# List-scheduled attention and two feed-forward layers on one core: costs read from a trace, and a rule that keeps GpSimd and VectorE's two-operand SBUF work apart

## The chip, the core and the metric

One core of a Trainium2 chip runs the whole program. The metric is device time in microseconds (us). The times below are those of the kernel before; the profile is of one execution. The engines are called PE (TensorE, matmuls), DVE (VectorE), ACT (ScalarE), POOL (GpSimd) and SP (SyncE, which here only issues DMAs).

## The reference

Causal attention with 2 x 12 heads, 448 positions and 64 values per head, then two feed-forward layers, each 768 to 2048 to 768 on the 896 rows:

```python
scores = scale * np.matmul(q, k.transpose(0, 1, 3, 2))
scores = np.where(mask, -1000000000.0, scores)
attn = np.exp(scores - np.max(scores, axis=-1, keepdims=True))
attn = attn / (np.sum(attn, axis=-1, keepdims=True) + 1e-09)
x = np.matmul(attn, v)                  # heads side by side: 896 x 768
h = x @ w_in;  x = (h * np.clip(h + 3.0, 0.0, 6.0) / 6.0) @ w_out
h = x @ w2_in; y = (np.maximum(h, 0.0) + alpha * np.minimum(h, 0.0)) @ w2_out
```

## The kernel before

**Attention** is cut into 12 units (`attend`, line 273), each of two heads ("sides") of one batch. For a unit PE makes the scores in four steps (`score(0)` to `score(2)` and `score_rest`, lines 286 to 302; tiles `s...` and `sl`). DVE applies the mask and takes the row minimum of the negated scores, seven times (`highest`, line 316, profile line 318). ACT exponentiates each of the seven pieces in place (`exps`, profile line 323). When all seven are there, DVE inverts the row sums (`invert`, lines 331 to 334), and POOL multiplies the seven pieces by the inverse in SBUF (line 338, tiles `el` and `e`): one instruction for `el` and six for the `e` pieces. PE then transposes the 16 blocks into four PSUM banks `t` (lines 345 and 353), each bank is copied to SBUF as a quarter of `a` by ACT or DVE (`copy`, line 374, profile line 375), and PE multiplies by V into `o` (line 387). A unit's `o` is turned into the operands of the first layer by `take_x` (line 242): a copy, or sums and differences with other units (`combine`, profile line 239), each split into a high part rounded by ACT (`split`, line 221) and a low part, a difference made by DVE (line 222).

**The layers** use a seven-product scheme for 2 x 2 blocks in place of eight, and each product is three matmuls (high x high, high x low, low x high) in `three` (line 397; instruction line 404). One such step is three matmuls of 448 columns. The steps of `w_in` (line 411) number 8 groups x 7 products x 3, those of `w_out` (line 496) 192 per layer. All 720 of both layers are chained in one fixed order (`chain="moe"`). The weights arrive as 64-bit integers' words: `convert` (line 196) takes two ACT steps (lines 205 and 207) and two DVE steps (lines 209 and 212) for each tile of 768 columns. In `w_in` the converted tiles are added and subtracted (`sums`, line 418) and split (`both`, lines 429 and 430). The first group's first product is `a <- a1 x b11`: its operands `b1100`, `b1101` and `b1102` come from units 1, 3 and 5.

**The order of all work** is made by a list scheduler (`Plan.solve`, line 94) before anything is emitted. Every step names its engine (or two, for copies) and a cost in us; `LAG` (line 60) is what an engine's result takes to reach another engine. The scheduler keeps a clock for each engine, and takes again and again the step that can start first; among equals, the one that is due first. Buffers of each class are limited (`SLOTS`, line 541), and a step waits for a free one. The result is one order for each engine's queue; at run time every engine works through its queue in that order, and semaphores hold an instruction until its operands are there. So a cost that is wrong in the table moves instructions, and nothing else. The first costs of interest:

```python
LAG = {PE: 0.20, DVE: 0.10, ACT: 0.10, POOL: 0.12, SP: 0.0}
                    t = max(clock[e], o.ready[e])
                        key = (round(t, 2), o.due, o.index)
            o.out = o.end = clock[e] = t + dict(o.on)[e]
            op([(ACT, 0.62), (DVE, 0.64)], copy, reads=[t], writes=[(a, i)])
            op((POOL, 0.26 + 0.00088 * cols), lambda _, view=view, u=u: nc.gpsimd.tensor_scalar(
```

Of the kernel before, what the change touches and what calls it, by code (L numbers as in the profile page):

```python
# [36 lines left out]
def f32(t):  # L37
    return t.bitcast(F32)
# [21 lines left out]
LAG = {PE: 0.20, DVE: 0.10, ACT: 0.10, POOL: 0.12, SP: 0.0}  # L60
# [3 lines left out]
class Plan:  # L64
# [28 lines left out]

    def solve(self, slots, strict, overlay):
# [21 lines left out]
        clock, landed = dict.fromkeys(LAG, 0.0), 0.0  # L116
# [69 lines left out]
class Kernel:  # L186
# [9 lines left out]
    def convert(self, src):  # L196
# [4 lines left out]
        def words(k):  # L201
            return raw.tile.rearrange("p (n two) -> p n two", two=2)[:, :, k]

        op((SP, 0.06), lambda e: nc.sync.dma_start(out=raw.tile, in_=src), writes=[(raw, "l"), (raw, "h")]).load = (1.6, 2.8)
        op((ACT, 0.85), lambda e: nc.scalar.activation(f32(w.tile), f32(words(1)), AF.Copy, scale=2.0 ** -112),  # L205
           reads=[(raw, "h")], writes=[w])
        op((ACT, 0.87), lambda e: nc.scalar.activation(  # L207
# [3 lines left out]
           reads=[w], writes=[(raw, "l")])  # L211
        op((DVE, 0.87), lambda e: nc.vector.scalar_tensor_tensor(  # L212
            out=w.tile, in0=w.tile, scalar=0x80000000, in1=words(0), op0=ALU.bitwise_and, op1=ALU.bitwise_or),
           reads=[(raw, "l")], writes=[w])
        return w

    def split(self, cls, name, cols, src, key, ps=False):

        nc, op = self.nc, self.plan.op
        hi, lo = Buf(cls, name + "h", cols, F32R), Buf(cls, name + "l", cols, F32R)  # L220
        op((ACT, 0.11 + 0.00094 * cols), lambda e: nc.scalar.copy(hi.tile, src()), reads=[key], writes=[hi])  # L221
        op((DVE, 0.14 + 0.00094 * cols), lambda e: nc.vector.tensor_sub(lo.tile, src(), f32(hi.tile)),  # L222
           reads=[key, hi], writes=[lo])
        return hi, lo

    def copy(self, out, src, key, cols):
        nc = self.nc

        def emit(e):
            (nc.scalar.copy if e == ACT else nc.vector.tensor_copy)(out.tile, src())  # L230

        self.plan.op([(ACT, 0.11 + 0.00096 * cols), (DVE, 0.10 + 0.00104 * cols)], emit, reads=[key], writes=[out])

    def combine(self, name, in0, in1, key0, key1, subtract=True):
# [4 lines left out]
        self.plan.op((DVE, 0.55), lambda e: f(t.tile, in0(), in1()), reads=[key0, key1], writes=[t])  # L239
        return t  # L240

    def take_x(self, layer, c, blk, ps):
# [11 lines left out]
        elif low:  # L254
            x[layer, "b11", j] = self.split("u", "b11" + n, S, src, ps)
# [3 lines left out]
        elif blk:  # L259
            x[layer, "b22", j] = self.split("u", "b22" + n, S, src, ps)  # L260
# [5 lines left out]
        else:  # L266
            x[layer, "b21", j] = self.split("u", "b21" + n, S, src, ps)
# [5 lines left out]
    def attend(self, n, c, blk, due):  # L273
        nc, op, d = self.nc, self.plan.op, self.dram
        kq, v = Buf("kq", "kq", S + 4 * P, F32), Buf("v", "v", 8 * D, F32)
        op((SP, 0.06), lambda e: nc.sync.dma_start(out=kq.tile, in_=d["kq"][n]), writes=[kq]).load = (1.6, 2.2)
        op((SP, 0.06), lambda e: nc.sync.dma_start(out=v.tile, in_=d["v"][n]), writes=[v]).load = (1.6, 1.2)
# [21 lines left out]
        op((PE, 0.24), score(0), reads=[kq], writes=[(s01[0], 0), (s01[1], 0)], also=[*e01])  # L299
        op((PE, 0.45), score(1), reads=[kq], writes=[(s01[0], 1), (s01[1], 1)])  # L300
        op((PE, 0.66), score(2), reads=[kq], writes=[*s2], also=[*e2])
        op((PE, 0.77), score_rest, reads=[kq], writes=[sl], also=[el])
# [9 lines left out]
        for t, key, off, e, u, cols in todo:  # L312
# [14 lines left out]
            op((DVE, 0.09 + 0.00102 * cols), highest, reads=[key], writes=[part, (small, u)])  # L327
# [8 lines left out]
        op((DVE, 0.36), invert, reads=[(small, 7 + u) for u in range(7)], writes=[(small, 14)])  # L336
        for view, part, u, cols in views:
            op((POOL, 0.26 + 0.00088 * cols), lambda _, view=view, u=u: nc.gpsimd.tensor_scalar(  # L338
# [25 lines left out]
        for i, blocks in enumerate(banks):  # L364
# [6 lines left out]
            op((PE, 0.50), emit, reads=list(dict.fromkeys((el, 0) if i == 3 else key(kc, i, side) for kc, i, side in blocks)),  # L371
# [5 lines left out]
            op([(ACT, 0.62), (DVE, 0.64)], copy, reads=[t], writes=[(a, i)])  # L377

        o = Buf("ps", "o")
        for kc, us in enumerate((0.77, 0.55, 0.34, 0.13)):  # L380
# [30 lines left out]
    def w_in(self, layer, m, src, due):  # L411
# [5 lines left out]
        def sums(out, oh, in0, h0, in1, h1, f, reads):  # L417
            op((DVE, 0.50), lambda _: f(out.tile[:, oh], f32(in0.tile[:, h0]), f32(in1.tile[:, h1])),  # L418
               reads=reads, writes=[(out, oh.start)])
# [7 lines left out]
        def both(name, cols, src, keys):  # L427
            hi, lo = Buf("w", name + "h", DM, F32R), Buf("w", name + "l", DM, F32R)
            op((ACT, 0.08 + 0.00094 * cols), lambda _: nc.scalar.copy(hi.tile[:, 0:cols], src()), reads=keys, writes=[hi])  # L429
            op((DVE, 0.14 + 0.00095 * cols), lambda _: nc.vector.tensor_sub(lo.tile[:, 0:cols], src(), f32(hi.tile[:, 0:cols])),  # L430
               reads=[*keys, hi], writes=[lo])
# [27 lines left out]
        def finish(h, mm, blk, until, ps=None):  # L459
# [3 lines left out]
            if layer == 0:  # L463
                op((ACT, 0.54), lambda _: nc.scalar.activation(t.tile, src(), AF.Relu, bias=0.5, scale=1.0 / 6.0),  # L464
# [4 lines left out]
            else:  # L469
                op((ACT, 0.54), lambda _: nc.scalar.activation(t.tile, src(), AF.Relu, scale=-1.0),  # L470
# [48 lines left out]
    def store(self, layer, c, blk, ps):  # L519
# [3 lines left out]
        self.plan.op((SP, 0.06), lambda _: nc.sync.dma_start(out=out[c, :, blk, :], in_=o.tile), reads=[o])  # L523

    def build(self):
# [5 lines left out]
        op((SP, 0.06), lambda _: nc.sync.dma_start(out=self.alpha, in_=d["alpha"]), writes=[alpha], due=start + 20.0).load = (1.6, 0.4)  # L531
# [124 lines left out]
```

## Time and profile before

| what | us |
|---|---|
| three timed runs | 552.08, 551.77, 548.56 |
| median of the runs | 551.77 |
| the profiled execution | 548.4 |
| its span, first to last instruction | 546.6 |
| PE busy in the span | 528.2 |
| DVE busy | 428.0 |
| ACT busy | 337.9 |
| POOL busy | 53.5 |

The profiled execution took 1.8 us more than its span. Stretches are given in us from the start of the span. Attention fills the stretch up to about 109; the first layer's `w_in` follows up to about 206, its `w_out` up to about 322, then the second layer in the same way. A busy PE in the table is not a PE at full pace: its clock is granted at one of two levels, and the strip and the table of stretches show the mean of the granted clock, 1.00 being full.

### The profile page before, as it was taken

How to read it: one execution, taken by the hardware profiler on the slowest of the kernel's cores; microseconds unless marked ns; L12 is line 12 of the kernel's file. 1: busy time of each engine (PE TensorE's matmuls, PEld its weight loads, DVE VectorE, ACT ScalarE, POOL GpSimd, SP SyncE). 2: the span in 40 equal slices, each digit the busy share in tenths (PEclk: the TensorE clock that was granted, in tenths of full speed). 3: DMA queues.
4: the chain of work that ended last, by engine and by line, in shares of the span. 5: the costliest groups of instructions: out<-in, count | busy, mean ns of one | idle time of the engine just before them, and what ended most of it. 6: DMA issues, size and time to landing. Idle time of an engine off the chain costs nothing.

```text
span 546.6 us, 7448 instructions
## 1 busy us (share of the span) xinstructions
PE 528.2 (97%) x2712; PEld 459.8 (84%) x2712; DVE 428.0 (78%) x773; ACT 337.9 (62%) x627; POOL 53.5 (10%) x97
## 2 busy tenths in 40 slices
PE   5977999999999999999999999999999999999997
PEld 2544566799999999999999998999999999999996
DVE  4888898799999999997641499999999999751002
ACT  5787688756767899946532366676779985631000
POOL 3454573500000000000000000000000000000000
PEclk9879899999999999999999999999999999999999
DMA  8534332003434343356231012334334344730002
GB/s 312 192 98 166 117 112 76 1 20 108 157 119 140 123 145 115 120 201 225 93 111 62 0 59 65 128 124 146 117 121 145 111 144 149 238 118 1 0 17 84
DMA packets 14581, 62.61 MB, mean 115 GB/s; under 512 B 1745, under 2 KB 3281, under 8 KB 14545
## 3 DMA queue, kind: packets, MB, share of 16 engines
q1 hardware_dynamic: 14544, 62.14, 33.1%
q8 instruction: 21, 0.34, 0.2%
q14 instruction: 16, 0.12, 0.1%
HBM read 59.38 MB, written 2.75 MB: 114 GB/s over the span
## 4 chain that ended last, share of the span: by engine, by line
PE 91%; DVE 3%; POOL 3%; ACT 1%; issue 1%; DMA 1%; POOLq 0%; DVEq 0%
PE y L404 42%; PE a L404 20%; PE c L404 10%; PE b L404 5%; PE o L387 5%; PE t L353 3%; PE s L291 3%; POOL e L338 3%; PE sl L297 2%; PE t L345 1%; DMA kq<-kq 1%; ACT e L323 1%; DVE e L318 1%; DVE t L239 0%; POOL el L338 0%
## 5 line engine op out<-in xcount | busy, mean ns | idle before, releaser
L207 ACT ACTIVATE raw<-raw 128x768 uint32<-128x768 uint32 x64 | 58.8, 919 | 40.6 <-DMA raw<-w2i 18.8
L205 ACT ACTIVATE wf<-raw 128x768 f32<-128x768 f32 x64 | 57.1, 903 | 16.1 <-PE y L404 13.5
L209 DVE SCALAR_TENSOR_TENSOR raw<-wf,raw 128x768 uint32<-128x768 uint32 x64 | 61.5, 962 | 2.6 <-ACT wf L205 2.6
L212 DVE SCALAR_TENSOR_TENSOR wf<-wf,raw 128x768 uint32<-128x768 uint32 x64 | 61.2, 957 | 1.5
L222 DVE TENSOR_TENSOR wol<-wf,woh 128x768 fp32r<-128x768 f32 x32 | 30.4, 953 | 21.4 <-PE y L404 17.3
L338 POOL TENSOR_SCALAR e<-e,small 128x384 f32<-128x384 f32 (+2 forms) x72 | 43.6, 628 | 0.0
L230 DVE COPY o<-y 128x448 f32<-128x448 f32 x10 | 6.2, 624 | 43.3 <-PE y L404 43.3
L221 ACT CAST woh<-wf 128x768 fp32r<-128x768 f32 x32 | 26.3, 836 | 21.1 <-PE y L404 13.6
L323 ACT ACTIVATE e<-e,small 128x384 f32<-128x384 f32 (+2 forms) x72 | 35.7, 501 | 2.9 <-DVE small L318 2.7
L353 PE MATMUL t<-ident,e 128*128 128x128 f32 x144 | 25.9, 303 | 4.9 <-POOL e L338 4.9
L318 DVE CUSTOM_DVE_ANT_0 e<-s,mask 128x384 f32<-128x384 f32 (+2 forms) x72 | 26.7, 417 | 2.5 <-PE s L291 1.8
L387 PE MATMUL o<-a,v 128*64 128x448 f32 (+3 forms) x192 | 28.2, 401 | 0.0
L387 PEld LDWEIGHTS o<-a,v 128*64 128x64 f32 (+1 forms) x192 | 13.4, 137 | 17.3 <-issue 10.2
L353 PEld LDWEIGHTS t<-ident,e 128*128 128x128 f32 x144 | 19.2, 155 | 7.8 <-POOL e L338 7.7
L430 DVE TENSOR_TENSOR s12l<-s,s12h 128x768 fp32r<-128x768 f32 x16 | 15.2, 951 | 12.4 <-PE y L404 12.4
L418 DVE TENSOR_TENSOR s<-wf 128x384 f32<-128x384 f32 x32 | 17.8, 555 | 8.3 <-PE y L404 7.7
L291 PE MATMUL s<-kq 64*128 64x384 f32 (+2 forms) x144 | 22.3, 426 | 0.0
L291 PEld LDWEIGHTS s<-kq 64*128 64x128 f32 x144 | 13.0, 197 | 9.9 <-issue 5.6
L429 ACT CAST s12h<-s 128x768 fp32r<-128x768 f32 x16 | 13.3, 832 | 11.5 <-DVE s L418 10.9
L375 DVE COPY a<-t 128x512 f32<-128x512 f32 x23 | 15.5, 686 | 6.1 <-PE t L353 3.0
L375 ACT COPY a<-t 128x512 f32<-128x512 f32 x25 | 13.9, 590 | 9.7 <-PE t L353 8.2
L464 ACT ACTIVATE r<-g 128x448 f32<-128x448 f32 x24 | 13.7, 572 | 8.1 <-DVE g L457 8.1
(649 smaller groups left out, 1648.9 us busy)
## 6 DMA issues: line engine op xcount, KB each, us to landing
raw<-w1i SPq DMA_DIRECT2D x16, 768.0 KB, 5.0
raw<-w1o SPq DMA_DIRECT2D x16, 768.0 KB, 5.2
raw<-w2i SPq DMA_DIRECT2D x16, 768.0 KB, 4.3
raw<-w2o SPq DMA_DIRECT2D x16, 768.0 KB, 4.6
kq<-kq SPq DMA_DIRECT2D x12, 480.0 KB, 4.7
v<-v SPq DMA_DIRECT2D x12, 256.0 KB, 2.8
y_t<-o SPq DMA_DIRECT2D x12, 224.0 KB, 1.9
alpha<-alpha SPq DMA_DIRECT2D x1, 8.0 KB, 6.7
```

The lines of the kernel that those rows point to most:

```text
L205: op((ACT, 0.85), lambda e: nc.scalar.activation(f32(w.tile), f32(words(1)), AF.Copy, scale=2.0 ** -112), reads=[(raw, "h")], writes=[w])
L207: op((ACT, 0.87), lambda e: nc.scalar.activation(words(0), words(0), AF.Copy, bias=-0.4999, scale=2.0 ** -29 * (1 - 2.0 ** -16)), writes=[ ...
L209: op((DVE, 0.87), lambda e: nc.vector.scalar_tensor_tensor(out=words(0), in0=w.tile, scalar=3, in1=words(0), op0=ALU.logical_shift_left, o ...
L212: op((DVE, 0.87), lambda e: nc.vector.scalar_tensor_tensor(out=w.tile, in0=w.tile, scalar=0x80000000, in1=words(0), op0=ALU.bitwise_and, o ...
L222: op((DVE, 0.14 + 0.00094 * cols), lambda e: nc.vector.tensor_sub(lo.tile, src(), f32(hi.tile)), reads=[key, hi], writes=[lo])
L291: nc.tensor.matmul(t.tile[:, off:off + (i + 1) * P], lhsT=kq.tile[rows, S + i * P:S + (i + 1) * P], rhs=kq.tile[rows, 0:(i + 1) * P], star ...
L318: nc.vector.tensor_tensor_reduce(out=view(), in0=t.tile[:, off:off + cols], in1=self.mask[:, at:at + cols], scale=-SCALE, scalar=3.0e38, o ...
L323: nc.scalar.activation(view(), view(), AF.Exp, bias=small.tile[:, u:u + 1], scale=-1.0, accum_out=small.tile[:, 7 + u:8 + u])
L338: op((POOL, 0.26 + 0.00088 * cols), lambda _, view=view, u=u: nc.gpsimd.tensor_scalar(view(), view(), small.tile[:, 14 + u:15 + u], 1.0, A ...
L353: return lambda t: nc.tensor.transpose(t.tile[:, at:at + P], src.tile[:, off:off + P], self.ident)
L387: nc.tensor.matmul(o.tile[side * D:(side + 1) * D, 0:cols], lhsT=v.tile[rows, (2 * kc + side) * D:(2 * kc + side + 1) * D], rhs=a.tile[row ...
L404: nc.tensor.matmul(out, lhsT=lhs.tile[:, w], rhs=rhs.tile, start=start and lhs is hi and rhs is xh, stop=stop and lhs is lo, skip_group_ch ...
```

## The change

The costs and lags in the plan are replaced by others. A step can carry a mark, `port`: all POOL steps have it, and those DVE steps whose two tensor operands both lie in SBUF (the two of `convert`, `sums`, the low parts in `both`, and `split` when its source is not in PSUM). The scheduler keeps one more clock, `port`, and starts a marked step of DVE or POOL only when the last marked one has ended in its plan. No semaphore is added; the mark acts on the order alone. Operations, buffers and their numbers stay. Of the costs a few lines are shown.

```diff
-LAG = {PE: 0.20, DVE: 0.10, ACT: 0.10, POOL: 0.12, SP: 0.0}
+LAG = {PE: 0.20, DVE: 0.12, ACT: 0.15, POOL: 0.10, SP: 0.04}
...
-    def op(self, on, emit, reads=(), writes=(), due=FAR, chain=None, also=()):
+    def op(self, on, emit, reads=(), writes=(), due=FAR, chain=None, also=(), port=False):
 
         o = Op(on if isinstance(on, list) else [on], emit, due)
+        o.port = port or o.on[0][0] == POOL
...
-        clock, landed = dict.fromkeys(LAG, 0.0), 0.0
+        clock, landed, port = dict.fromkeys(LAG, 0.0), 0.0, 0.0
...
                     t = max(clock[e], o.ready[e])
+                    if o.port and e in (DVE, POOL):
+                        t = max(t, port)
...
             o.out = o.end = clock[e] = t + dict(o.on)[e]
+            if o.port and e in (DVE, POOL):
+                port = o.end
...
         op((DVE, 0.87), lambda e: nc.vector.scalar_tensor_tensor(
             out=words(0), in0=w.tile, scalar=3, in1=words(0), op0=ALU.logical_shift_left, op1=ALU.bitwise_or),
-           reads=[w], writes=[(raw, "l")])
+           reads=[w], writes=[(raw, "l")], port=True)
...
-            op([(ACT, 0.62), (DVE, 0.64)], copy, reads=[t], writes=[(a, i)])
+            op([(ACT, 0.48), (DVE, 0.605)], copy, reads=[t], writes=[(a, i)])
```

On DVE, behind the inversion for unit 2 (the unit whose tiles `e_295` to `e_313` POOL multiplies next), before the change: `s_283` and `s_376` are sums of weight tiles, `raw` a weight tile under conversion. The accumulator read that follows each `L318` row is left out.

```order
L333 TENSOR_SCALAR small<-small 128x7
L334 RECIPROCAL small<-small 128x7
L318 ISA e_340,small<-s_333,mask 128x128
L318 ISA e_341,small<-s_334,mask 128x128
L222 TENSOR_TENSOR b1100l<-o,b1100h 128x448
L418 TENSOR_TENSOR s_283<-s_283,wf 128x384
L239 TENSOR_TENSOR t_372<-b_246,o 128x448
L418 TENSOR_TENSOR s_376<-wf,s_283 128x384
L418 TENSOR_TENSOR s_376<-wf 128x384
L209 SCALAR_TENSOR_TENSOR raw<-wf,raw 128x768
L375 COPY a<-t 128x512
L333 TENSOR_SCALAR small<-small 128x7
```

The same place after the change, from the inversion for unit 2 on; the rows of line 323 are unit 3's score work, and the line numbers are those of the changed file (five higher here):

```order
L338 TENSOR_SCALAR small<-small 128x7
L339 RECIPROCAL small<-small 128x7
L323 ISA e_306,small<-s_304,mask 128x384
L323 ISA e_307,small<-s_305,mask 128x384
L244 TENSOR_TENSOR t_338<-b_252,o 128x448
L323 ISA e_343,small<-s_333,mask 128x256
L323 ISA e_344,small<-s_334,mask 128x256
L323 ISA e_343,small<-s_333,mask 128x128
L323 ISA e_344,small<-s_334,mask 128x128
L227 TENSOR_TENSOR b1100l<-o,b1100h 128x448
L217 SCALAR_TENSOR_TENSOR wf<-wf,raw 128x768
L380 COPY a<-t 128x512
```

Six DVE instructions for unit 3's scores and two with a PSUM operand now stand where three weight sums and a conversion stood.

On PE, behind unit 3's scores (`s_333`, `s_334`) and ahead of unit 2's transposes, before the change:

```order
L291 MATMUL s_333<-kq 128x128
L291 MATMUL s_334<-kq 128x128
L404 MATMUL a<-b1100h,a1h 128x448
L404 MATMUL a<-b1100l,a1h 128x448
L404 MATMUL a<-b1100h,a1l 128x448
L345 MATMUL t<-ident,el 128x2x64
L353 MATMUL t<-ident,e_295 128x128
```

After the change the transposes follow the scores at once:

```order
L296 MATMUL s_333<-kq 128x128
L296 MATMUL s_334<-kq 128x128
L350 MATMUL t<-ident,el 128x2x64
L358 MATMUL t<-ident,e_222 128x128
L358 MATMUL t<-ident,e_264 128x128
```

The first product of the layer (`b1100`) has left this place; it now stands on PE behind the last scores of unit 11, and the second (`b1101`) behind unit 10's first product with V, where before it stood ahead of unit 4's transposes.

On ACT, at the copies of unit 11's four banks `t`, before the change (the other two copies are on DVE):

```order
L221 CAST b2202h<-o 128x448
L221 CAST t202h<-t_1190 128x448
L375 COPY a<-t 128x512 x2
L221 CAST t302h<-t_1224 128x448
L221 CAST b2102h<-o 128x448
```

After the change all four are on ACT:

```order
L226 CAST t401h<-t_1114 128x448
L226 CAST b2202h<-o 128x448
L380 COPY a<-t 128x512 x4
L226 CAST t202h<-t_1151 128x448
L226 CAST t302h<-t_1170 128x448
```

Over all 12 units ACT has 32 of the 48 copies instead of 25, and DVE 16 instead of 23.

## Rows read from the trace of the kernel before

**Rows 1.** The page: span, busy time of the engines, clock strip (40 slices, tenths)
```profile
span 546.6 us, 7448 instructions
...
PE 528.2 (97%) x2712; PEld 459.8 (84%) x2712; DVE 428.0 (78%) x773; ACT 337.9 (62%) x627; POOL 53.5 (10%) x97
...
PEclk9879899999999999999999999999999999999999
```

**Rows 2.** Busy time by stretch: PE, PEld, DVE, ACT, POOL, granted clock, DMA share, GB/s
```profile
8.00:15.00 7.00, 4.67 (x29) 2.70 (x26) 5.41 (x30) 6.70 (x27) 3.01 (x7) 1.00 1.02 420
15.00:31.00 16.00, 15.15 (x89) 8.86 (x87) 14.86 (x39) 12.13 (x27) 5.11 (x9) 0.89 0.52 185
31.00:46.00 15.00, 11.12 (x58) 6.94 (x58) 11.91 (x25) 10.76 (x26) 11.10 (x14) 0.77 0.15 48
46.00:60.00 14.00, 10.57 (x61) 6.94 (x59) 11.37 (x38) 9.89 (x31) 4.74 (x7) 0.88 0.58 202
60.00:91.00 31.00, 31.00 (x217) 18.35 (x216) 28.02 (x97) 26.14 (x79) 18.95 (x35) 1.00 0.35 107
91.00:107.00 16.00, 16.00 (x112) 11.79 (x111) 13.18 (x42) 13.37 (x39) 8.08 (x15) 1.00 0.00 1
107.00:206.00 99.00, 99.00 (x493) 91.07 (x494) 96.86 (x152) 72.88 (x118) 0.00 (x0) 1.00 0.33 112
206.00:543.00 337.00, 336.91 (x1661) 311.29 (x1659) 244.78 (x357) 184.04 (x282) 0.00 (x0) 1.00 0.32 109
```

**Rows 3.** Waits of PE, whole span, then 16 to 60: total, times, longest
```profile
PE t L353 <- POOL e L338: 4.9, 8, 1.2
...
PE a L404 <- DVE b1101l L222: 2.1, 1, 2.1
PE a L404 <- DVE b1100l L222: 2.1, 1, 2.1
PE t L345 <- POOL el L338: 1.4, 1, 1.4
...
PE t L353 <- POOL e L338: 3.9, 6, 1.2
```

**Rows 4.** Timeline of POOL: start, us; units 0, 2, 3 and 4
```profile
12.60 2.75 POOL L338 TENSOR_SCALAR e<-e,small 128x384 f32<-128x384 f32 x6
...
32.07 4.52 POOL L338 TENSOR_SCALAR e<-e,small 128x384 f32<-128x384 f32 x6
...
38.92 5.35 POOL L338 TENSOR_SCALAR e<-e,small 128x384 f32<-128x384 f32 x6
...
53.05 4.13 POOL L338 TENSOR_SCALAR e<-e,small 128x384 f32<-128x384 f32 x6
```

**Rows 5.** Timeline of DVE beside unit 2's multiplications
```profile
32.12 0.55 DVE L418 TENSOR_TENSOR s<-s,wf 128x384 f32<-128x384 f32 x1
...
33.12 0.89 DVE L418 TENSOR_TENSOR s<-wf,s 128x384 f32<-128x384 f32 x1
```

**Rows 6.** Waits of ACT from 8 to 107, the copies of `a`
```profile
ACT a L375 <- PE t L353: 8.2, 10, 2.2
...
ACT a L375 <- PE t L345: 1.3, 2, 0.7
```

**Rows 7.** Groups by line and shape: busy us, mean ns of one, idle before
```profile
L207 ACT ACTIVATE raw<-raw 128x768 uint32<-128x768 uint32 x64 | 58.8, 919 | 40.6 <-DMA raw<-w2i 18.8 <-DMA raw<-w2o 11.7 <-DMA raw<-w1o 9.7
...
L375 DVE COPY a<-t 128x512 f32<-128x512 f32 x23 | 15.5, 686 | 6.1 <-PE t L353 3.0 <-PE t L345 2.7
...
L375 ACT COPY a<-t 128x512 f32<-128x512 f32 x25 | 13.9, 590 | 9.7 <-PE t L353 8.2 <-PE t L345 1.3
...
L429 ACT CAST s12h<-s 128x768 fp32r<-128x768 f32 x16 | 13.3, 832 | 11.5 <-DVE s L418 10.9 <-PE y L404 0.6
```

**Rows 8.** The chain that ended last: unit 11's `o` and three steps: start, us
```profile
106.98 2.44 PE o L387 x14
...
112.05 1.82 PE a L404 x9
```

More of the change, by code (lines that the diff above doesn't have):

```diff
@@ L220, in split @@
         hi, lo = Buf(cls, name + "h", cols, F32R), Buf(cls, name + "l", cols, F32R)
-        op((ACT, 0.11 + 0.00094 * cols), lambda e: nc.scalar.copy(hi.tile, src()), reads=[key], writes=[hi])
-        op((DVE, 0.14 + 0.00094 * cols), lambda e: nc.vector.tensor_sub(lo.tile, src(), f32(hi.tile)),
-           reads=[key, hi], writes=[lo])
+        op((ACT, (0.0 if ps else 0.04) + 0.00094 * cols), lambda e: nc.scalar.copy(hi.tile, src()), reads=[key], writes=[hi])
+        op((DVE, 0.065 + 0.00105 * cols), lambda e: nc.vector.tensor_sub(lo.tile, src(), f32(hi.tile)),
+           reads=[key, hi], writes=[lo], port=not ps)
         return hi, lo
@@ L230, in emit @@
             (nc.scalar.copy if e == ACT else nc.vector.tensor_copy)(out.tile, src())
-        self.plan.op([(ACT, 0.11 + 0.00096 * cols), (DVE, 0.10 + 0.00104 * cols)], emit, reads=[key], writes=[out])
+        self.plan.op([(ACT, 0.00094 * cols), (DVE, 0.065 + 0.00105 * cols)], emit, reads=[key], writes=[out])
     def combine(self, name, in0, in1, key0, key1, subtract=True):
@@ L238, in combine @@
         f = nc.vector.tensor_sub if subtract else nc.vector.tensor_add
-        self.plan.op((DVE, 0.55), lambda e: f(t.tile, in0(), in1()), reads=[key0, key1], writes=[t])
+        self.plan.op((DVE, 0.54), lambda e: f(t.tile, in0(), in1()), reads=[key0, key1], writes=[t])
         return t
@@ L266, in take_x @@
         else:
[L267 removed]
+            x[layer, "b21", j] = self.split("u", "b21" + n, S, src, ps, True)
             t2 = f["t2", j]
@@ L297, in score_rest @@
             nc.tensor.matmul(sl.tile[:, 0:S], lhsT=kq.tile[:, S + 3 * P:], rhs=kq.tile[:, 0:S], start=True, stop=True)
[L299 to L302, printed above, removed]
+        op((PE, 0.32), score(0), reads=[kq], writes=[(s01[0], 0), (s01[1], 0)], also=[*e01])
+        op((PE, 0.44), score(1), reads=[kq], writes=[(s01[0], 1), (s01[1], 1)])
+        op((PE, 0.77), score(2), reads=[kq], writes=[*s2], also=[*e2])
+        op((PE, 0.90), score_rest, reads=[kq], writes=[sl], also=[el])
         todo = []
@@ L326, in attend @@
             part = (e, off)
-            op((DVE, 0.09 + 0.00102 * cols), highest, reads=[key], writes=[part, (small, u)])
+            op((DVE, 0.075 + 0.00106 * cols), highest, reads=[key], writes=[part, (small, u)])
             op((ACT, 0.28 + 0.00085 * cols), exps, reads=[(small, u)], writes=[part, (small, 7 + u)])
@@ L334, in invert @@
             nc.vector.reciprocal(r, r)
-        op((DVE, 0.36), invert, reads=[(small, 7 + u) for u in range(7)], writes=[(small, 14)])
+        op((DVE, 0.33), invert, reads=[(small, 7 + u) for u in range(7)], writes=[(small, 14)])
         for view, part, u, cols in views:
-            op((POOL, 0.26 + 0.00088 * cols), lambda _, view=view, u=u: nc.gpsimd.tensor_scalar(
+            op((POOL, 0.24 + 0.00083 * cols), lambda _, view=view, u=u: nc.gpsimd.tensor_scalar(
                 view(), view(), small.tile[:, 14 + u:15 + u], 1.0, ALU.mult, ALU.mult),
@@ L369, in emit @@
                     (rest(kc) if j == 3 else flip(kc, j, side))(t)
-            op((PE, 0.50), emit, reads=list(dict.fromkeys((el, 0) if i == 3 else key(kc, i, side) for kc, i, side in blocks)),
+            op((PE, 0.45), emit, reads=list(dict.fromkeys((el, 0) if i == 3 else key(kc, i, side) for kc, i, side in blocks)),
                writes=[t], also=[a])
@@ L417, in sums @@
         def sums(out, oh, in0, h0, in1, h1, f, reads):
-            op((DVE, 0.50), lambda _: f(out.tile[:, oh], f32(in0.tile[:, h0]), f32(in1.tile[:, h1])),
-               reads=reads, writes=[(out, oh.start)])
+            op((DVE, 0.47), lambda _: f(out.tile[:, oh], f32(in0.tile[:, h0]), f32(in1.tile[:, h1])),
+               reads=reads, writes=[(out, oh.start)], port=True)
         add, sub = nc.vector.tensor_add, nc.vector.tensor_sub
@@ L428, in both @@
             hi, lo = Buf("w", name + "h", DM, F32R), Buf("w", name + "l", DM, F32R)
-            op((ACT, 0.08 + 0.00094 * cols), lambda _: nc.scalar.copy(hi.tile[:, 0:cols], src()), reads=keys, writes=[hi])
-            op((DVE, 0.14 + 0.00095 * cols), lambda _: nc.vector.tensor_sub(lo.tile[:, 0:cols], src(), f32(hi.tile[:, 0:cols])),
-               reads=[*keys, hi], writes=[lo])
+            op((ACT, 0.04 + 0.00092 * cols), lambda _: nc.scalar.copy(hi.tile[:, 0:cols], src()), reads=keys, writes=[hi])
+            op((DVE, 0.065 + 0.00105 * cols), lambda _: nc.vector.tensor_sub(lo.tile[:, 0:cols], src(), f32(hi.tile[:, 0:cols])),
+               reads=[*keys, hi], writes=[lo], port=True)
             return hi, lo
```

26 lines of the change are left out of this document (13 added, 13 removed).

## The prediction

> **What bounds the kernel now.** The page first [rows 1]: PE is busy 528.2 of 546.6 us, and its strip of granted clocks is below full in the first five slices and 9 (full) in all the others. So little is left to win, and it lies at the front. The table of stretches shows where [rows 2]: from 60 us on PE is never idle (31.00 of 31.00, 16.00 of 16.00, 99.00 of 99.00, 336.91 of 337.00) at a clock of 1.00. The order of the 720 weight steps on PE is chained, so what follows attention takes the same PE time after the change: three steps of three matmuls take 1.82 us [rows 8], 0.608 each. The end moves only as far as the end of attention moves on PE, unless a new wait opens in the layers.
>
> Ahead of 60 us PE loses time in two ways. It waits: 0.85 us of 15 to 31, 3.88 of 31 to 46 and 3.43 of 46 to 60, together 8.2. And it is slow: the granted clock averages 0.77 and 0.88 in the last two [rows 2], which are stretches of 1.2 GHz among those of 2.4. The list of PE's waits gives the causes [rows 3]: 2.1 + 2.1 us for the low parts `b1100l` and `b1101l`, 4.9 + 1.4 for POOL, of which 3.9 fall between 16 and 60. 4.2 + 3.9 = 8.1 us, the 8.2 of the stretches.
>
> POOL's own rows say why it is late [rows 4]. Unit 0's six `e` pieces take 2.75 us, unit 2's 4.52, unit 3's 5.35, unit 4's 4.13: 1.8, 2.6 and 1.4 us more for the same instructions. Beside unit 2's stand DVE's weight sums, and one of them takes 0.89 us where another takes 0.55 [rows 5]. Both sides stretch, and the DVE instructions are those with both operands in SBUF.
>
> **The change part by part.** Nothing is added or removed; the costs decide the order.
>
> *A, the two early products.* On PE the first two products of the layer stood ahead of the transposes of units 2 and 4, and PE stood still before each until DVE, late with its queue, had made a low part. They now stand behind unit 11's scores and unit 10's first product with V, some 40 us later, when units 1 and 3 are long done. 2.1 + 2.1 = 4.2 us go. The product moved does not become cheaper, it is done later without a wait. What is late next there is POOL, which is B.
>
> *B, POOL.* Behind unit 2's inversion DVE now has six instructions on unit 3's scores and two with a PSUM operand, then the conversion. POOL's work there should fall back to the 2.75 us of unit 0, and the 3.9 us go. As to bounds: nothing goes if the queues drift so that the same pairs meet; POOL's surplus of 1.8 + 2.6 + 1.4 = 5.8 us for three units is the most. I take the 3.9 that PE really waited.
>
> The traces show the stretching as above. The Trainium skill, page "SBUF — State Buffer", section "Who interferes with whom", states that GpSimd and VectorE share one pair of ports under an exclusive lock, that a VectorE instruction with two SBUF inputs contends with a GpSimd instruction that reads SBUF, and that the later one blocks fully. The rows of POOL and of the weight sum agree. The rule also speaks against the change: a lock that is exclusive costs the sum of both in either order, so keeping them apart turns POOL's wait into one of DVE. That is the second rival below.
>
> *C, the clock.* With no gaps I expect 31 to 60 to run at the full level, as everything from 60 on does. PE was busy 11.12 us at 0.77 and 10.57 at 0.88: 0.23 x 11.12 + 0.12 x 10.57 = 2.6 + 1.3 = 3.8 us. Bounds: nothing, or the whole deficit of the stretches, 0.23 x 15 + 0.12 x 14 = 5.1. The low clock between 15 and 31 stays: unit 0 must still come through the softmax before PE has much to do.
>
> *D, the start.* Part of unit 2's scores moves ahead of unit 0's product with V. PE had no wait in the table there besides that for `b1100l`, so I count 0; it gives DVE and ACT unit 2 earlier, and at most the 2.33 us that PE idles from 8 to 15 [rows 2] bound it.
>
> *E, ACT.* Seven bank copies move from DVE (0.686 us each) to ACT (0.590), 4.8 us off DVE and 4.1 onto ACT [rows 7]. Against that, ahead of unit 11's last copy ACT's queue has two conversions fewer (0.919) and two wide casts fewer (0.832), and two narrow ones, which I price at 0.590: 1.8 + 1.7 + 1.2 = 4.7. From 8 to 107 ACT was busy 6.70 + 12.13 + 10.76 + 9.89 + 26.14 + 13.37 = 79.0 us of 99 [rows 2], so it has 78.4 to do there now. Unit 11's product with V began at 107 [rows 8]; PE has five weight steps fewer ahead of it (8 before, 3 now, 3.0 us, done later). A gain of G at the end thus means that ACT does 78.4 us in 99 - 3.0 - G. For G = 11.9 (A, B and C) it must be busy 93% of the time, against 80% now. Of its 20.0 us of idle time 8.2 + 1.3 = 9.5 are waits for the banks `t` [rows 6], PE's stalls passed on. With those alone gone it would take 78.4 + 10.5 = 88.9, and G = 7.1. I take 10, between 7.1 and 11.9 and nearer to the upper, since other waits of ACT (for DVE's minima, for `o`) hang on the same stalls. So E is -1.9.
>
> Sum: 4.2 + 3.9 + 3.8 + 0 - 1.9 = 10.0 us. From 548.4, the profiled execution (its span and 1.8 us), that makes 538.4. The runs' median of 551.77 lies 3.4 above that execution, which is among the fastest; a new median should lie likewise, so I forecast 551.8 - 10.0 = 541.8.
>
> *The layers.* No new wait is counted there. DVE is busy 96.86 of 99.00 us from 107 to 206 [rows 2], nearly the whole of the stretch, so whatever DVE brings late into `w_in` stays late. By the order, DVE has 18 two-operand SBUF instructions ahead of unit 11's last score work in place of 28, and five low parts fewer; these come later. The cover is DVE's idle time: 1.59 + 1.14 + 3.09 + 2.63 + 2.98 + 2.82 = 14.3 us from 8 to 107 and 2.1 to 206, 16.4 together. With the end of `w_in` 10 us earlier and 4.8 us of copies gone, 16.4 - 10.0 + 4.8 = 11.2 us of idle may remain. Each us above that is a us for PE.
>
> **The rivals.**
>
> *1. ACT becomes the bound, in part.* At the 84% that ACT was busy from 60 to 91, where PE never waited, 78.4 / 0.84 = 93.3 us and G = 96.0 - 93.3 = 2.7: 549.1. For: it gets copies of DVE just where it is needed. Against: it was then kept waiting by a PE that set the pace.
>
> *2. The lock moves the wait to DVE.* If DVE idles 16.4 us as now, 5.2 over what may remain, G = 4.8: 547.0. If POOL's 5.8 us come on top, G = -1.0: 552.8. For: DVE has no slack in `w_in`. Against: the new order has unmarked work for DVE to do beside POOL, as the rows show.
>
> *3. Slower: ACT's chain.* Copies of all four banks of a unit now stand in one queue with the exponentials of the next unit; if an exponential that waits for a minimum holds up the copies behind it, PE waits for `a`, the next scores come late, and ACT waits again. The price is what ACT's share falls to: at 78% it takes 100.5 us, G = -4.5: 556.3. It decides below 78.4 / 96.0 = 82%, and over the whole attention ACT is at 80% now. Against: half of its idle time has the causes that A and B remove.
>
> *4. The change does not do what it says.* Nothing at run time keeps POOL and DVE apart but the order. If they meet as before, B and C stay and A alone goes: G = 4.2, 547.6.
>
> **How the numbers follow.** The forecast (G from 7 to 14) gets 0.68, more than 14 gets 0.02, rival 1 0.11, rival 2 0.10, rival 3 0.05, rival 4 0.04. For the range: the low end takes C at 5.1, B at 5.8 and E at 0, 15.1, and a little of D: 535.5. The high end is 549.5, which takes in rivals 1 and 4 and half of rival 2; about 0.12 is left outside. A measurement of this kernel can tell about 1% from no change, 5.5 us. Faster by more: 0.68 + 0.02 and some 0.07 of the milder cases of rivals 1, 2 and 4, 0.77. Slower by more: most of rival 3, 0.04. The rest, 0.19, is the same.
>
> **What would show it.** A: no wait of PE for `b1100l` or `b1101l`. B: six `e` pieces in about 2.8 us for units 2 to 4, and PE's waits for POOL down to those of unit 0, 2.4 us. C: a clock of 1.00 from about 25 us on. E: ACT busy about 91% up to unit 11's last copy. The layers: PE at its full time from attention's end to the last matmul. I am wrong if PE waits for `a` or for ACT in attention (rivals 1 and 3), if PE waits in `w_in` for weights (rival 2), or if the six pieces still take over 4 us (rival 4).

## The result, and the profile after

The changed kernel took 537.47 us in the median of its runs (537.12 to 538.58), the kernel before 551.29 (548.56 to 552.08). The ratio is 0.9761, with a 95% interval of 0.9724 to 0.9799: 2.4% faster. The forecast of 541.8 was 4.3 us too high, within its range. The profiled execution went from 548.4 to 537.68 us and its span from 546.6 to 535.8, 10.8 us. (The times of one kernel lie in groups up to 3 us apart: the 19 of the kernel before that stand beside e1 at 548.2 to 548.9 or at 551.2 to 552.0.)

The page of the profile after: span, busy time and instructions of the engines, the clock strip, and the chain that ended last, by engine.

```profile
span 535.8 us, 7453 instructions
...
PE 524.8 (98%) x2712; PEld 454.1 (85%) x2712; DVE 417.6 (78%) x762; ACT 337.6 (63%) x638; POOL 44.8 (8%) x97
...
PEclk9899999999999999999999999999999999999999
...
PE 79%; DVE 14%; DMA 3%; issue 2%; ACT 1%; POOL 0%; DVEq 0%; SPq 0%; ACTq 0%; POOLq 0%
```

POOL is busy 8.7 us less for the same 97 instructions, and one slice of the strip shows less than 9 where three did. The chain has changed too: now DVE has 14% of it. The kernel before had this line:

```profile
PE 91%; DVE 3%; POOL 3%; ACT 1%; issue 1%; DMA 1%; POOLq 0%; DVEq 0%
```

The stretches after, with the columns of [rows 2]:

```profile
15.00:31.00 16.00, 16.00 (x103) 10.35 (x104) 13.16 (x43) 13.97 (x35) 7.79 (x16) 0.90 0.39 133
31.00:46.00 15.00, 15.00 (x103) 8.85 (x103) 14.05 (x51) 14.98 (x46) 7.03 (x15) 1.00 0.57 181
46.00:60.00 14.00, 14.00 (x104) 8.44 (x103) 11.43 (x38) 13.71 (x41) 6.89 (x14) 1.00 0.33 108
60.00:91.00 31.00, 31.00 (x218) 19.39 (x219) 28.48 (x95) 28.91 (x86) 17.74 (x35) 1.00 0.18 59
...
107.00:206.00 99.00, 99.00 (x482) 89.92 (x482) 97.52 (x152) 75.18 (x127) 0.00 (x0) 1.00 0.37 126
```

From 15 us on PE is never idle in attention, and from 31 on its clock is full. But look at the last row: PE is busy 99.00 of 99.00 us as before, and did 482 matmuls where it did 493 [rows 2]. All waits of PE in the span:

```profile
PE sl L302 <- DMA kq<-kq: 4.1, 1, 4.1
PE t L350 <- POOL el L343: 2.0, 1, 2.0
PE t L358 <- POOL e L343: 0.9, 2, 0.7
PE a L409 <- DVE g L462: 0.2, 1, 0.2
```

The two waits for low parts [rows 3] are gone, and POOL's share is 2.9 us, all of it in unit 0. POOL's six `e` pieces of units 2, 3 and 4, which took 4.52, 5.35 and 4.13 us [rows 4], in its timeline (start, us):

```profile
27.65 2.75 POOL L343 TENSOR_SCALAR e<-e,small 128x384 f32<-128x384 f32 x6
...
34.64 2.75 POOL L343 TENSOR_SCALAR e<-e,small 128x384 f32<-128x384 f32 x6
...
41.62 2.74 POOL L343 TENSOR_SCALAR e<-e,small 128x384 f32<-128x384 f32 x6
```

The chain after, at the end of attention, in both layers' `w_in` and in the last `w_out` (start, us, what):

```profile
90.43 1.27 PE o L392 x12
91.70 2.05 PE c L409 x9
...
101.20 3.72 PE a L409 x18
...
162.54 1.82 PE a L409 x9
...
479.84 40.33 PE y L409 x199
```

Attention's last product ends at 91.70, where it ended at 109.42 [rows 8]. That is 17.7 us, of which 5 x 0.608 = 3.0 are weight steps put behind it: attention gained 14.7. The span gained 10.8, so the layers gave back 3.9. The chain shows a part of it: three steps take 1.86 us (half of 3.72) in places and 1.82 in others.

### The profile page after: what moved, and what is told of

It is laid out like the page before. It is cut to its first block, busy times and chain, and to the rows that moved or that the text cites. A ratio compares the mean times of both kernels' runs of the same rounds, so it can differ in the third digit from the quotient of the medians.

```text
span 535.8 us, 7453 instructions
## 1 busy us (share of the span) xinstructions
PE 524.8 (98%) x2712; PEld 454.1 (85%) x2712; DVE 417.6 (78%) x762; ACT 337.6 (63%) x638; POOL 44.8 (8%) x97
## 3 DMA queue, kind: packets, MB, share of 16 engines
HBM read 59.38 MB, written 2.75 MB: 116 GB/s over the span
## 4 chain that ended last, share of the span: by engine, by line
PE 79%; DVE 14%; DMA 3%; issue 2%; ACT 1%; POOL 0%; DVEq 0%; SPq 0%; ACTq 0%; POOLq 0%
PE y L409 41%; PE a L409 13%; PE c L409 6%; PE o L392 5%; PE s L296 4%; PE t L358 3%; PE b L409 3%; DVE g L477 2%; DMA raw<-w2i 2%; PE sl L302 2%; DVE wf L217 2%; DVE raw L214 2%; PE t L350 1%; DVE s L423 1%; DVE s34l L435 1%
## 5 line engine op out<-in xcount | busy, mean ns | idle before, releaser
L343 POOL TENSOR_SCALAR e<-e,small 128x384 f32<-128x384 f32 (+2 forms) x72 | 33.7, 488 | 0.0
L392 PE MATMUL o<-a,v 128*64 128x448 f32 (+3 forms) x192 | 25.8, 393 | 0.0
L392 PEld LDWEIGHTS o<-a,v 128*64 128x64 f32 (+1 forms) x192 | 11.3, 135 | 16.1 <-issue 7.1
L423 DVE TENSOR_TENSOR s<-wf 128x384 f32<-128x384 f32 x32 | 17.7, 554 | 8.0 <-PE y L409 7.2
L358 PE MATMUL t<-ident,e 128*128 128x128 f32 x144 | 22.8, 284 | 0.9 <-POOL e L343 0.9
L296 PEld LDWEIGHTS s<-kq 64*128 64x128 f32 x144 | 12.6, 194 | 10.2 <-issue 6.2
L358 PEld LDWEIGHTS t<-ident,e 128*128 128x128 f32 x144 | 17.8, 146 | 2.3 <-POOL e L343 1.8
L380 ACT COPY a<-t 128x512 f32<-128x512 f32 x32 | 17.0, 591 | 2.3 <-PE t L350 1.3
L302 PE MATMUL sl<-kq 128*128 128x448 f32 x24 | 13.2, 634 | 4.1 <-DMA kq<-kq 4.1
L477 DVE SCALAR_TENSOR_TENSOR g<-r,alpha,g 128x448 f32<-128x448 f32 x24 | 16.4, 682 | 0.0
L235 ACT COPY g<-c 128x448 f32<-128x448 f32 x14 | 7.5, 534 | 13.3 <-PE c L409 13.3
```

The costliest lines, as they stand in the source:

```text
L296: nc.tensor.matmul(t.tile[:, off:off + (i + 1) * P], lhsT=kq.tile[rows, S + i * P:S + (i + 1) * P], rhs=kq.tile[rows, 0:(i + 1) * P], star ...
L343: op((POOL, 0.24 + 0.00083 * cols), lambda _, view=view, u=u: nc.gpsimd.tensor_scalar(view(), view(), small.tile[:, 14 + u:15 + u], 1.0, A ...
L358: return lambda t: nc.tensor.transpose(t.tile[:, at:at + P], src.tile[:, off:off + P], self.ident)
L392: nc.tensor.matmul(o.tile[side * D:(side + 1) * D, 0:cols], lhsT=v.tile[rows, (2 * kc + side) * D:(2 * kc + side + 1) * D], rhs=a.tile[row ...
L477: op((DVE, 0.56), lambda _: nc.vector.scalar_tensor_tensor(out=h.tile, in0=t.tile, scalar=self.alpha[:, mm:mm + 1], in1=src(), op0=ALU.mul ...
```

## The experiments

Two theories stood against each other. The first is the prediction's: the gain comes from the port rule (B) and from the late first products (A), with the clock behind both. The rival is that it comes from the earlier scores, which the prediction priced at nothing (D), and so from the part of the table that moves them: the costs of DMA loads. The old plan has 0.06 us for an issue on SP and `load = (1.6, 2.2)` for `kq` (1.6 us to the start, 2.2 for the bytes, one load after another); the new one has 0.45 and `(2.1, 1.2)`. All medians are of runs on the same chip as the runs of before that stand beside them; e1, e2, e3 and e5 shared one chip, so did e4, e6, e7 and e8, and so did e9, e10, e12 and e13. Where times of two chips are compared, the ratios to the kernel before say more than the times.

**e1, the costs without the port rule** (the kernel after with one line changed):

```diff
-        o.port = port or o.on[0][0] == POOL
+        o.port = False
```

> The new costs and lags without the port rule. By the order the early product stands behind unit 8's work (so the waits of PE for b1100l and b1101l, 4.2 us, should be gone), but of the 3.4 us of VectorE's queue that follow each of the 12 inversions 8.0 us in all are instructions with two SBUF operands, against 12.6 before and 4.1 after the change. Theory (both parts are needed): GpSimd's six pieces take over 3.5 us for some units, about half of B and C stays, 543 to 545. Rival (the costs alone do it): 537 to 539, with the six pieces at 2.8. Rival (only the port rule counts): 548 or more.

Measured: 542.83 us against 551.17, ratio 0.9878 (0.984 to 0.9917). POOL is late again, in its timeline for units 1 and 2:

```profile
19.16 5.22 POOL L343 TENSOR_SCALAR e<-e,small 128x384 f32<-128x384 f32 x6
...
29.61 3.74 POOL L343 TENSOR_SCALAR e<-e,small 128x384 f32<-128x384 f32 x6
```

Without the rule 8.3 us of gain remain: it cannot be the main cause, though the kernel after is 3.6 to 5.4 us quicker with it (539.23 and 537.47 in its two series).

**e2, the port rule with the old costs** (the kernel before, with the mark, the scheduler's `port` clock and the marked steps):

```diff
+                    if o.port and e in (DVE, POOL):
+                        t = max(t, port)
```

> The port rule with the old costs and lags. By the order 4.6 us of two-operand work follow the inversions, nearly as few as after the change, but the first product still stands behind unit 3's scores. Theory: GpSimd's pieces fall to about 2.8 us for most units, the wait for b1100l stays (2 us), the one for b1101l goes, 542 to 546. Rival (the port rule is the whole gain): 537 to 539. Rival (the costs are the whole gain): 549 to 552.

Measured: 546.98 us against 551.17, ratio 0.9938 (0.9901 to 0.9976). The rule alone is worth 4.2 us by the medians and 3.4 by the ratio; its runs spread from 542.37 to 550.97. With e1's 8.3 that makes some 12 of the 13.8 between the medians, but the parts don't simply add, as e12 below shows.

**e3, the late products alone** (the kernel before, with the first weight step held behind unit 11's scores):

```diff
+        if n == 2 * KIN - 1:
+            self.plan.last["moe"] = o
```

> The kernel before with one edge more in its plan: the first weight step waits for unit 11's scores. Everything else as before, 11.6 us of two-operand work behind the inversions. Theory: the two waits of 2.1 us go and no more than part of the low clock, 546 to 548; GpSimd's six pieces still take over 4 us for units 2 to 4. Rival (the early products hold up the whole chain, and POOL's stretch hides under other work once they are gone): 541 or less. Rival (POOL takes up what the products leave, no gain): 550 to 552.

Measured: 551.48 us against 551.17, ratio 1.0021 (0.9992 to 1.005): nothing. PE's waits say why:

```profile
PE t L355 <- POOL e L340: 6.4, 10, 1.8
PE t L347 <- POOL el L340: 5.5, 3, 2.4
```

The waits for `b1100l` and `b1101l` are gone, and the waits for POOL have gone from 6.3 us [rows 3] to 11.9. What PE no longer waited for DVE it waited for POOL at the next transposes.

**e9, port rule and late products together, old costs** (both edits above):

> The kernel before with the port rule and with the first weight step held behind unit 11's scores: A and B of the prediction, with the old costs. By the order 4.0 us of two-operand work follow the inversions; unit 2's scores still stand behind unit 1's products with V. Theory (A pays once B is there, and alone it does not): 541 to 544, no wait of PE for b1100l, GpSimd's six pieces at 2.8 us. Rival (the early loads and scores are what frees the chain, so A and B together give no more than B alone): 546 to 548.

Measured: 546.59 us against 551.8, ratio 0.9899 (0.9831 to 0.9967), 0.4 us from e2's median. A adds nothing to B either. PE's waits:

```profile
PE t L352 <- POOL el L345: 3.7, 2, 2.5
PE t L360 <- POOL e L345: 2.8, 5, 0.9
PE sl L302 <- DVE small L325: 1.8, 1, 1.8
```

**e10, the new load costs alone** (the kernel before; the same for `v`, `raw`, `alpha` and the stores):

```diff
-        op((SP, 0.06), lambda e: nc.sync.dma_start(out=kq.tile, in_=d["kq"][n]), writes=[kq]).load = (1.6, 2.2)
+        op((SP, 0.45), lambda e: nc.sync.dma_start(out=kq.tile, in_=d["kq"][n]), writes=[kq]).load = (2.1, 1.2)
```

> The kernel before with the new costs of SyncE's loads and stores alone (0.45 to issue, 2.1 to start, shorter after that). By the order this alone brings unit 2's scores ahead of unit 0's product with V, takes the first weight step behind unit 8, and leaves 5.0 us of two-operand work behind the inversions, without any port rule. Theory (D, the early scores, is the root of much of the gain): 542 to 545. Rival (the engines' own costs and the port rule are the gain): 548 to 551.

Measured: 541.95 us against 551.8, ratio 0.9828 (0.9763 to 0.9893): some 10 of the 12.6 us that the whole change gained on that chip (e13, below). Its timeline of PE at the first scores of unit 2, and its stretches:

```profile
17.39 0.92 PE L297 MATMUL sl<-kq 128*128 128x448 f32 x2
```

```profile
31.00:46.00 15.00, 13.33 (x93) 8.33 (x92) 13.19 (x46) 12.19 (x42) 9.38 (x19) 1.00 0.55 201
46.00:60.00 14.00, 14.00 (x100) 8.44 (x99) 12.92 (x44) 12.91 (x38) 6.01 (x13) 1.00 0.43 124
```

Unit 2's scores begin at 17.39 us. In the kernel before they begin here (its PE timeline):

```profile
23.85 1.02 PE L297 MATMUL sl<-kq 128*128 128x448 f32 x2
```

Their `kq` was issued at 8.91 us there, and the trace has it landed 7.6 us later, at 16.5. The old plan counted loads one behind another, behind three of 768 KB, and believed in a landing at 20.60 on its own clock (which starts with the first issue, 0.74 in the trace); the new plan also counts one behind another, but at less for each, and believes in 13.45. So the scores stood behind other work for 7.3 us with their operands there, and the new plan takes them as soon as they are. From 31 to 60 PE did 193 matmuls where it did 119 [rows 2], at the full clock, without any port rule.

**e12, everything new but the load costs** (the kernel after, with the `-` values of e10):

```diff
-        op((SP, 0.45), lambda e: nc.sync.dma_start(out=kq.tile, in_=d["kq"][n]), writes=[kq]).load = (2.1, 1.2)
+        op((SP, 0.06), lambda e: nc.sync.dma_start(out=kq.tile, in_=d["kq"][n]), writes=[kq]).load = (1.6, 2.2)
```

> The changed kernel with the old costs of SyncE's loads and stores. By the order unit 2's scores go back behind unit 1's transposes, the first weight step back ahead of unit 2's transposes, and 6.9 us of two-operand work follow the inversions although the port rule is on. Theory (D as the root): 543 to 548. Rival (port rule and engine costs suffice): 537 to 540.

Measured: 552.09 us against 551.8, ratio 1.0015 (0.998 to 1.0051): with the rule, the new engine costs and all of POOL's six pieces at 2.75 us, nothing is gained. And yet e2, with the rule and the old costs throughout, gained 4.2: with the old load costs, the new engine costs take that away again. The profiled execution took 557.63 us, 5.5 above the median, so its rows show more than the usual loss. Its PE waits, a piece of POOL's timeline (unit 2), its stretches, and SP's issues of `kq`:

```profile
PE sl L302 <- DMA kq<-kq: 5.1, 2, 4.1
PE t L358 <- POOL e L343: 4.0, 9, 0.7
PE a L409 <- DVE b1100l L227: 2.7, 1, 2.7
PE t L350 <- POOL el L343: 2.4, 2, 1.3
```

```profile
32.01 2.75 POOL L343 TENSOR_SCALAR e<-e,small 128x384 f32<-128x384 f32 x6
```

```profile
31.00:46.00 15.00, 13.21 (x81) 8.27 (x82) 10.89 (x32) 12.52 (x35) 6.72 (x14) 0.89 0.19 60
...
60.00:91.00 31.00, 28.35 (x171) 17.26 (x167) 24.77 (x84) 24.12 (x72) 13.45 (x28) 0.94 0.39 141
```

```profile
27.12 2.78 SPq L281 DMA_DIRECT2D kq<-kq  x2
46.00 2.78 SPq L281 DMA_DIRECT2D kq<-kq  x2
```

POOL is as quick as in unit 0, and yet PE waits for it. The likely reason is that a unit's scores begin so late that its whole softmax is late. The loads of later units go out late too (a row with x2 is two loads, one behind the other): unit 6's at 46.00. There are only two buffers for `kq`, so a load waits until an earlier unit's scores are done. In the kernel after, the loads of units 4 to 6 go out here:

```profile
24.66 0.38 SPq L281 DMA_DIRECT2D kq<-kq  x1
29.34 0.33 SPq L281 DMA_DIRECT2D kq<-kq  x1
35.84 0.33 SPq L281 DMA_DIRECT2D kq<-kq  x1
```

**e6, the early scores held back** (the kernel after; all scores of units 2 and 3 wait for the second and for the last step of unit 1's product with V):

```diff
+        if n in (2, 3):
+            for o in self.plan.ops[-4:]:
+                o.before.add(self.gives[1, 1 if n == 2 else 3])
```

> The changed kernel with the scores of units 2 and 3 held back to where they stood before (behind unit 1's second and fourth product with V), all costs and the port rule kept. Theory (term D is worth more than the 0 it was given: with unit 2's scores 6 us earlier the softmax never starves PE afterwards): 541 to 545, PE waits for GpSimd again at unit 2. Rival (D is worth nothing, as predicted): 537 to 539.

Measured: 544.14 us against 548.57, ratio 0.9899 (0.9824 to 0.9974); span 539.4 against 535.8. Unit 2's scores begin at 24.95 in its PE timeline, and a wait of PE is new. It is for DVE; the wait for GpSimd at unit 2 that was expected did not come:

```profile
24.95 1.02 PE L303 MATMUL sl<-kq 128*128 128x448 f32 x2
```

```profile
PE sl L303 <- DVE small L327: 1.9, 1, 1.9
```

The late start of two units alone costs 3.6 us by the spans, and 4.9 to 6.7 by the medians (against the two series of the kernel after, 539.23 and 537.47, taken beside other runs of before). It is a part of what e12 lost, not the whole; the rest fits the later loads above, which were not tried alone.

**e7, the first products early** (the kernel after, with the first two weight steps put ahead of unit 2's and unit 4's transposes):

```diff
+        if self.cols in (1, 2):
+            for i in range(4):
+                self.flips[2 * self.cols, i].before.add(o)
```

> The changed kernel with the first two weight steps held ahead of the transposes of units 2 and 4, as before the change. Costs and port rule are kept. Theory (a weight step that waits for VectorE costs its wait only where the rest keeps up; here it does): 541 to 545, with waits of PE for b1100l or a1l. Rival (the place of the product does not matter, as the kernel before with late products showed no gain): 537 to 539.

Measured: 549.25 us against 548.57, ratio 0.9983 (0.9939 to 1.0027). The gain is gone, but the run doesn't tell why: the scheduler answered by taking unit 3 ahead of unit 2, and a new load wait came with that, 3.2 us at 63 (its PE waits show 7.3 for `kq`, of which 4.0 are the start's). It is inconclusive on A.

**e4, the copies back on DVE** (the kernel after, old cost of the bank copies; ACT then has 19 of the 48, DVE 29):

```diff
-            op([(ACT, 0.48), (DVE, 0.605)], copy, reads=[t], writes=[(a, i)])
+            op([(ACT, 0.62), (DVE, 0.64)], copy, reads=[t], writes=[(a, i)])
```

> The changed kernel with the old costs of the bank copies alone (0.62 on ScalarE, 0.64 on VectorE). By the order ScalarE then has 19 of the 48 copies and VectorE 29, against 32 and 16, and 2.8 us of two-operand work follow the inversions. Theory (ScalarE at 95% carries what it can; which engine copies is a matter of balance): 539 to 542. Rival (ScalarE's load costs 1.9 us, term E; without it the time falls): 535 to 537. Rival (the true copy cost is most of the gain): 543 or more.

Measured: 543.74 us against 548.57, ratio 0.9884 (0.9816 to 0.9952), 4.5 to 6.3 above the two series of the kernel after. PE has new waits, all for DVE:

```profile
PE a L409 <- DVE t401l L227: 1.3, 1, 1.3
PE o L392 <- DVE a L380: 1.2, 1, 1.2
...
PE c L409 <- DVE s12l L435: 0.8, 3, 0.3
PE a L409 <- DVE a1l L435: 0.7, 1, 0.7
```

So ACT's 32 copies are worth having; DVE, not ACT, is the engine without room. Most of the loss is not in attention: by the count below, attention ends 1.1 us later than in the kernel after, and the matmuls of the first `w_in` take 4.4 us more than as many do there. The profile also has 2.3 us from the slower pace that the last section tells of.

**e5 and e8, slack in the layers.** Both look for the 3.9 us given back. In the second `w_in` of the kernel after, several of PE's first matmuls on a PSUM bank start only some 0.05 us after DVE or ACT has emptied it, so PE waited for that. The new costs of these steps are close to their measured times and leave no slack. e5 corrects one cost, e8 pads all of those that empty banks:

```diff
-                op((DVE, 0.56), lambda _: nc.vector.scalar_tensor_tensor(
+                op((DVE, 0.595), lambda _: nc.vector.scalar_tensor_tensor(
```

```diff
-        self.plan.op([(ACT, 0.00094 * cols), (DVE, 0.065 + 0.00105 * cols)], emit, reads=[key], writes=[out])
+        self.plan.op([(ACT, more + 0.00094 * cols), (DVE, more + 0.065 + 0.00105 * cols)], emit, reads=[key], writes=[out])
...
-            self.copy(t, out_of(ps), ps, S)
+            self.copy(t, out_of(ps), ps, S, 0.06)
```

> The changed kernel with one cost corrected: the activation step of the second layer on VectorE at 0.595 us in place of 0.56, which is its start-to-start time in the trace. Attention and the first layer keep their order. Theory (the small waits of PE in the second layer's w_in come from a plan that believes VectorE faster than it is): about 2 us less, 535 to 536.5, and no wait of PE over 0.1 us from 320 to 415. Rival (those waits come from elsewhere, or the matmuls' own pace gives them back): 537 to 538.

> The changed kernel with the costs of the steps that empty a PSUM bank in w_in padded (0.58 and 0.60 in place of 0.54 and 0.56 on VectorE, 0.06 more for the copies), attention in the same order. Theory (PE's waits of 0.1 to 0.4 us in w_in come from a plan with no slack there, since the old costs were 0.02 to 0.1 us too long and the new ones are exact): those waits go, 1.5 to 2.5 us less, 535 to 536. Rival (they do not depend on it, or the matmuls' pace hides it): 537 to 539.

Measured: e5 541.33 us against 551.17, ratio 0.9854 (0.981 to 0.9899); e8 541.29 against 548.57, ratio 0.9827 (0.9756 to 0.9897), its fastest run 537.52. Neither beats the kernel after, and the theory behind e5 fell: the small waits stayed. They can be counted from the starts of PE's matmuls in the trace, by what exceeds 0.203 us from one start to the next where they are 0.209 or more apart: in the second `w_in` 2.1 us in the kernel after (0.5 before), 2.0 in e5 and 1.3 in e8. So the padding did shorten them, but in e8, too, PE did 503 matmuls from 311 to 415 us, as many as in the kernel after. What made both slow in their profiles is mostly something else, 2.3 us in the last `w_out` of each. The chain of e5 there:

```profile
479.99 40.09 PE y L409 x194
```

The kernel after has 199 of the same matmuls in 40.33 us (its chain, above): 0.2027 us each against 0.2066, at the same granted clock of 1.00.

**e13, the kernel after again**, unaltered, beside e10 and e12:

> The changed kernel once more, unaltered, beside the three others on one chip. Theory (the matmuls of the weight steps have two paces, 0.203 and 0.207 us, and an execution falls into the one or the other from stall to stall): 537 to 542, with runs some 2.3 us apart, and a stretch of w_out that is wholly at the one pace or the other. Rival (the changed kernel is always at the quick pace in w_out): all runs within 537 to 539.

Measured: 539.23 us (538.36 to 544.08) against 551.8, ratio 0.9798 (0.9726 to 0.987). The gain holds in a second series, 12.6 us. The rival fell, and the two paces were there. The chain in the first `w_out`, in this run and then in the first profile of the same kernel:

```profile
250.00 40.09 PE y L409 x194
```

```profile
249.89 40.13 PE y L409 x198
```

**Attention by itself.** The profiles allow a count that is free of what the layers did: the end of attention's last product on PE, less 0.608 us for each weight step done ahead of it. It is 104.6 us in the kernel before, 105.2 in e3, 105.9 in e12, 98.2 in e9, 97.8 in e2, 94.0 in e10, 93.4 in e1, 93.3 in e6, 91.0 in e4, and 89.9 and 89.4 in the two profiles of the kernel after (one profile each). The load costs alone bring 10.6 of the 14.7 us, the rule alone 6.8, and the rule with the new engine costs brings nothing where the old load costs stay.

## Why the prediction came near, and where it was wrong

The total was right to 1 us in the profiled execution (10.0 forecast, 10.7 measured), and that is luck: attention gained 14.7 us where 10.0 were forecast, and the layers gave back 3.9 where nothing was. (A reading at the start is off too, without effect on the sum: of the first five slices of the strip only the second, third and fifth show less than 9.)

**B held as a mechanism.** The six pieces are back at 2.75 us, and PE's waits for POOL between 16 and 60 us, 3.9 before, are gone. The Trainium skill (page "SBUF — State Buffer", section "Who interferes with whom") states that GpSimd and VectorE share one pair of ports under an exclusive lock. The rows agree in that the pieces stretch only beside DVE's two-operand work: all 17 of POOL's multiplications in the kernel before that took over 0.06 us longer than the shortest of their shape overlap with such an instruction. Rival 2, which made of it an equal loss on DVE, fell: DVE's busy time from 107 to 206 is 97.52 against 96.86, and PE's list of waits has none there (the small stalls that the list does not show come below). Rival 4 (the two meet as before) fell by the same pieces. But B does not stand alone: e2 has it for 4.2 us, e12 has six pieces in 2.75 us and gains nothing.

**C held.** From 31 to 60 the clock is 1.00 and PE busy for 29.0 of 29.0 us; the low clock between 15 and 31 stayed, as forecast. Its 3.8 us were not measured by themselves.

**A failed as a term of the sum.** The 4.2 us were counted as gone beside B's 3.9, as if the two waits were independent. e3 and e9 show that a wait taken from DVE is one for POOL at the next transposes. In the order of the kernel before, the early products were a sign of a softmax that was late, not its cause; in the new order A has no clean test (e7).

**D was the step that failed most.** "PE had no wait in the table there besides that for `b1100l`, so I count 0" looked at PE, which had other units' work to do until unit 2 was needed. The price of a late start falls due later, as waits for POOL and DVE: e6 puts the early scores of units 2 and 3 at 3.4 us of attention and 3.6 of the span, above the bound of 2.33 that D had. e10 and e12 show that the load costs, of which the prediction says nothing, carry most of the change; what they bring beside those scores was not split further. One effect is in the order: in the 3.4 us of DVE work behind each of the 12 inversions (what POOL needs for a unit), two-operand SBUF work adds up to 12.6 us in the kernel before, 5.0 in e10 without any rule, and 4.1 after, counted from the queues at the new plan's costs. But this sum does not measure the gain: it is 8.0 in e1, which gains 8.3 us, 4.6 in e2, which gains 4.2, and 6.9 in e12, which gains none.

**E had the wrong sign.** It took 1.9 us off for ACT's load. ACT was busy 14.98 of 15.00 us from 31 to 46, and PE did not wait for it once; e4 shows that the old copy costs, with 13 of the copies back on DVE, lose 4.5 to 6.3 us. The step that failed is how far ACT could be filled. ACT worked at 94%, where the sum held it to about 91% and rival 1 to 84%, and both had these shares from a kernel in which ACT waited for PE. ACT's row up to the copies for unit 11:

```profile
8.00:88.00 80.00, 75.41 (x226) 0.98 0.40 139
```

Its waits for copies, 9.5 us [rows 6], are down to 2.1:

```profile
ACT a L380 <- PE t L350: 1.3, 1, 1.3
...
ACT a L380 <- PE t L358: 0.8, 3, 0.3
```

Rivals 1 and 3 fell with that.

**The layers failed too.** "No new wait is counted there", but they gave back 3.9 us. PE in 104 us of the second `w_in`, after:

```profile
311.00:415.00 104.00, 103.61 (x503) 1.00 0.34 114
```

The same in the kernel before:

```profile
324.00:428.00 104.00, 103.94 (x513) 1.00 0.34 114
```

Busy time differs by 0.3 us, but 10 matmuls of 0.203 us are missing: 2.0 us. In 99 us of the first `w_in` it is 482 against 493, 11 x 0.203 = 2.2 us. Two things are in it, a slower pace of matmuls (last section) and waits of 0.1 to 0.4 us, the longer of them for PSUM banks. The starts of the matmuls in the trace tell them apart. The first `w_in` lost 1.9 us against the kernel before: some 400 matmuls at 0.004 us more, 1.6, and 0.3 of waits. The second lost 1.9: 60 matmuls at the slower pace, 0.2, and 1.7 of waits. Both `w_out` took as long as before, 116.7 us each. So the new waits cost 2.0 us and the pace 1.8, and nothing here shows that the change sets the pace. In the second `w_in` the chain goes through DVE's queue, its work on the weights and on the banks alike; DVE was busy there 102.73 of the 104 us.

## What to carry to other kernels

In a kernel whose order comes from a planner, check every kind of cost against the trace, those of transfers first: a load believed to land 5 us late moved a whole unit, and the trace showed it only as waits for other engines. Before two waits of one engine are added up, ask whether the second would grow if the first went; a run that removes one alone tells. And count instructions in a stretch, not only busy time: an engine that is busy 99.00 of 99.00 us can still do 2% less.

## What the runs showed that was not expected

PE has two paces for the layers' matmuls of 448 columns at the same granted clock of 1.00: 0.2027 us (1.82 for nine) and 0.2067 (1.86 for nine). By the starts in the trace, at the second pace each matmul starts 0.2067 us after the one ahead; at the first, four in five start 0.2017 us after it, and every fifth 0.2067. The kernel before ran at the first throughout its profile; the kernel after ran at the second from 92.1 to 158.5 us, from 172.4 to 188.3 and from 400.8 to 413.2, e5 at the second for the whole last `w_out` (0.2066 from its chain row), where the kernel after ran at the first. Over the 576 matmuls of a `w_out` that is 2.3 us. A pace holds for tens to hundreds of matmuls, and the same instructions in the same order take either: the first `w_out` of the kernel after ran at the first pace in one profile and at the second in e13. Of the 28 `w_out` in the 14 profiles, 27 ran wholly at one pace, 19 at the first and 8 at the second; the other one (the first of e8) changed to the first pace at a wait, some ten matmuls in. In `w_in`, where PE has more waits, the pace changed within. So a single profile of one of these kernels can differ from the next by 2.3 us for each `w_out`, whatever was changed. Whether this is behind the 3 us between the times of one kernel is not shown: no profile was taken of an execution of the kernel before at 551 us or more. What decides the pace stayed open, and no run here tried it.
